# Memory rows issued from ScalarE and 64-row products as row pairs, in an interleaved two-block recurrent transformer kernel

## The chip, the cores and the metric

The kernel runs on one core of a Trainium2 chip. The metric is the device time of one execution in microseconds (us). The kernel before has a median of 1535.26 us over three runs (1532.87 to 1536.67). On this core TensorE multiplies matrices into PSUM (8 banks of 128 x 512 fp32), VectorE (DVE in the profile) and ScalarE (ACT) copy results out of PSUM and do the pointwise work, GpSimd (POOL) does a few small copies, and SyncE (SP) issues DMAs. Each engine runs its own list of instructions in order; semaphores order them between engines.

## The reference

The reference applies two blocks twice, x = x + A(layernorm(x)) and x = x + B(layernorm(x)), on 2048 rows of 448 numbers in bf16. Cut to what matters:

```python
def _A_ref(x, mem0, Wq, Wk, Wv, Wo, seg_len):          # 16 heads of 256, 8 memory rows, segments of 32
    mem = mem0
    for s in range(64):
        h = concat([mem, x[s*32:(s+1)*32]])            # 40 rows
        q, k, v = h @ Wq, h @ Wk, h @ Wv               # for each head
        p = softmax(where(mask, q @ k.T * scale, -1e9))
        o = (p @ v) @ Wo                               # summed over heads
        mem = o[:8]                                    # the next segment starts from these rows
        outs.append(o[8:])
def _B_ref(x, W_gate, W_up, W_down):                   # 448 -> 1792 -> 448
    return (relu(x @ W_gate) * (x @ W_up)) @ W_down
x = x + A(layernorm(x)); x = x + B(layernorm(x)); x = x + A(layernorm(x)); x = x + B(layernorm(x))
```

Block A is a recurrence over 64 segments: the memory rows of one segment are needed before the scores of the next can be formed.

## The kernel before, in words

At the start, for each head, the products M = Wq Wk^T and N = Wv Wo are formed and kept in SBUF, so that a segment needs T = h M, scores T h^T, a softmax, U = p h, and the output U N. The two applications of A run side by side as two layers, the second four segments (`LAG = 4`) behind the first. There are 68 steps, one for each segment; steps 0 to 3 and 64 to 67 have one layer, the others two. Step t does the following.

- `m_nat` (line 1203) copies the memory rows of the step before, which lie in `mv`, by DMA into `hK`, four DMAs of 8 rows x 224 (two layers, two halves; line 1216), and into `ride`, two DMAs of 16 rows x 224 (line 1223 adds them to the residual in every second step, on DVE). All six wait for `mv` alone. They are issued by `qdma` (line 893), which puts them on SP.
- `t_block` (line 982) forms T in 11 units of 4 to 6 head-columns, in three blocks of six, four and one unit. The 448 rows of the contraction are three tiles of 128 and one of 64. In the first two blocks the 64-row parts of all units come first (`first`, line 997), two units at a time: with two layers as four 64x64 products for each pair of columns (halves of rows times halves of columns), with one layer as two 64x128 products. Then come the 128-row parts of each unit (`rest`). Each unit fills one PSUM bank, which ACT or DVE empties by two copies, `TTm` (memory rows) and `TTs` (segment rows).
- `s_mem`, `p_t_mem`, `u_mem`, `un_mem` run the softmax, U and U N for the 8 memory rows only. Their result is `mv` (line 1178, DVE). `m_t` turns `mv` on TensorE, and DVE copies it to `hT`, where the next step's T reads it. This is the recurrence.
- `s_seg`, `seg_pt`, `u_seg` do the same for the 32 segment rows; `u_seg` ends in copies from PSUM to `U` (in the tile `big`) or `UTm`.
- In odd steps `un` forms the segment rows' output from `U`, `ln_b` normalises it (a DMA transpose `xBT<-xn` on SP is its last part), and `b_layer` runs block B.

The order of all work comes from a planner (`_Order.run`). Every operation gets a cost, a delay after its end (`lat`, in ns) and a due time. For TensorE operations the due time is looked up in a table `SLOT` that repeats every four steps. For the others it is worked back from the operations that follow, with corrections from `BIAS`. In the steady part (steps 8 to 63) the TensorE order is fixed by `SLOT` alone. The planner goes through time, gives each engine the operation that can start first (by due time where several can), chooses ACT or DVE for copies that may go to either, and assigns PSUM banks. Its costs for a DMA are 500 ns of SP and 2200 ns to landing for `qdma`, 120 ns of the issuing engine for the small loads that ACT issues at the start. Each engine's list is written out in this order and run strictly in it.

Of the kernel before, what the change touches and what calls it, by code (L numbers as in the profile page):

```python
# [24 lines left out]
DH = D // 2  # L25
# [508 lines left out]
def MM(out, lhsT, rhs, **kw):  # L534
    return (out, lhsT, rhs, kw)


class _Kernel:
# [354 lines left out]
    def qdma(self, name, fn, wr, rd=()):  # L893
        self.q.add("dma", ("sp",), {"sp": 500.0}, fn, rd, wr, name=name)

    def tile(self, pool, n):
        return _Tile(self, pool, n)

# [83 lines left out]
    def t_block(self, t, units):  # L982


        S = self
        pp, s = (t // 2) % 2, t % 2
        l0, l1 = S.layers(t)
        n = (l1 - l0) * KEYS
        rd = [("hTx", pp, s, l) for l in range(l0, l1)] + S.mkeys(pp, s, l0, l1) + (S.Mkeys if t == 0 else [])
        mov = lambda kt, h: S.hT[h, pp, kt, l0:l1, s, 0:KEYS]  # L990
        keys = lambda c, u0, m: [(nm, c, u0, half) for nm in ("TTm", "TTs") for half in ((0, 1) if c == 3 else (0,))]
        R = [S.tile("R", 1) for _ in units]
        pair = len(units) > 1
        block = str(S.BLOCKS.index(units))
        S.q.sub = block + "f"

        def first():
            out = []
            for a, b in zip(range(0, len(units), 2), range(1, len(units), 2)):
                for j in range(units[a][2]):  # L1000
                    for o, x in ((0, a), (0, b), (1, a), (1, b)) if l1 - l0 == 2 else ((-1, a), (-1, b)):
                        c, u0, m = units[x]
                        side, slot = S.PLACE[16 * c + u0 + j]
                        h, g = slice(64 * side, 64 * side + 64), slice(64 * o, 64 * o + 64) if o >= 0 else slice(0, 128)
                        out.append(MM(R[x].b()[g, j * n:j * n + n], S.M3[h, slot, g], mov(3, h), start=(j == 0), stop=False))
            return out

        if pair:
            S.mm(first, sum(u[2] for u in units[::2]) * S.pitch(n) + 25.0, rd, [r for x in R for r in x.res()] + [k for u in units for k in keys(*u)], mode=3 if l1 - l0 == 2 else 1)
        full = slice(0, 128)  # L1010
        for x, (c, u0, m) in enumerate(units):
            def rest(x=x, c=c, u0=u0, m=m):
                out = []
                for j in range(m):
                    v, o = R[x].b()[:, j * n:j * n + n], 16 * c + u0 + j
                    for kt in range(3):
                        out.append(MM(v, S.M[:, kt, o, :], mov(kt, full), start=(kt == 0 and not pair), stop=(kt == 2 and (j == m - 1 if pair else False))))
                    if not pair:
                        out.append(MM(v, S.M3[:, S.PLACE[o][1], :], mov(3, full), start=False, stop=True))
                return out  # L1020

            S.q.sub = block + "r"
            S.mm(rest, (3 if pair else 4) * m * S.pitch(n), rd, R[x].res() + ([] if pair else keys(c, u0, m)))
            S.t_copies(t, R[x], c, u0, m)
# [178 lines left out]
    def m_nat(self, t):  # L1203

        S = self
        pp, s = (t // 2) % 2, t % 2
        w = S.win(t - 1)
        for l in range(*S.layers(t)):
            if l == 1 and t == LAG:
                continue  # L1210
            for n in range(2):
                a, b = 64 * l + 32, 32 * n + 16 * w + 8 * l
                S.qdma(f"mk{l}{n}", lambda E, a=a, b=b, n=n: E.dma_start(S.hK[a:a + 8, pp, s, DH * n:DH * n + DH], S.mv[b:b + 8, :]),  # L1213
                       [("hKm", pp, s, l, n)], [("mem",)])
        S.q.sub = "x"
        p = (t - 2 - w) // 2
        if p in S.WTILES:
            for n in range(2):
                a, b = 64 + 16 * w, 32 * n + 16 * (1 - w)
                S.qdma(f"ride{n}", lambda E, a=a, b=b, n=n: E.dma_start(S.ride[a:a + 16, DH * n:DH * n + DH], S.mv[b:b + 16, :]), [("ride", w, n)], [("mem",)])  # L1220
            if w == 1:
                r = slice(64, 96)
                S.dve(lambda E: E.tensor_tensor(S.XB[r, (p + 1) % 2, :], S.ride[r, :], S.XA[r, p % 4, :], ALU.add), D,
                      [("ride", i, n) for i in range(2) for n in range(2)] + [("XA", p % 4, 1)], [("XB", (p + 1) % 2, 1)], base=(64, 64))
# [222 lines left out]
```

## Time and profile before

| | |
|---|---|
| median of 3 runs | 1535.26 us |
| the profiled execution | 1532.87 us, span 1531.1 us, mean granted TensorE clock 0.995 |
| PE busy | 1477.2 us, 41135 matmuls |
| DVE busy | 792.7 us |
| ACT busy | 784.5 us |
| DMAs `hK<-mv` and `ride<-mv` | 252 and 124, all issued from SP |

Busy time is the union of an engine's instructions. Instructions of a sequencer (marked with a q behind the engine, as in SPq) wait, branch or issue DMAs; they are not counted as busy. In a row of the timeline the first number is the start from the beginning of the span, the second the time that the merged instructions took, and what stands in brackets is how long the engine was idle before and what ended it.

### The profile page before, as it was taken

The page shows a single profiled execution, that of the slowest core. Times are in us where ns is not written, and L with a number is a line of the kernel's source. Part 1 is how long each engine was busy: PE and PEld are TensorE (multiplying, and loading weights), DVE is VectorE, ACT ScalarE, POOL GpSimd, SP SyncE. Part 2 cuts the span into 40 slices and gives each one's busy share as a digit, 9 for nine tenths or more (in the row PEclk, how much of TensorE's full clock was granted, in tenths as well). Part 3 has the DMA queues.
Part 4 walks back from the last instruction along what each step waited for, and adds up shares of the span by engine and source line. Part 5 has one row for each costly group of instructions (what it writes and reads, how often), then busy time and mean ns, then how long its engine had stood idle before and what let it go on. Part 6 is the DMA issues. An engine that isn't in the chain of part 4 may idle for free.

```text
span 1531.1 us, 88674 instructions
## 1 busy us (share of the span) xinstructions
PE 1477.2 (96%) x41135; PEld 1158.3 (76%) x41135; DVE 792.7 (52%) x2173; ACT 784.5 (51%) x2516; POOL 112.6 (7%) x259
## 2 busy tenths in 40 slices
PE   6999899999999999999999999999999999999998
PEld 2577777878787787878787787878788787878775
DVE  6544535545454555545555554545454564555554
ACT  6633554555545555554555455554555455554433
POOL 4000000000000000000000000000000000000000
PEclk9999999999999999999999999999999999999999
DMA  9741101111110100101010101111010110001010
GB/s 222 184 127 29 17 15 22 22 17 19 21 22 17 23 18 17 21 18 23 16 24 17 23 21 16 19 22 22 17 24 18 21 22 17 18 20 20 17 23 12
DMA packets 137761, 48.24 MB, mean 32 GB/s; under 512 B 125736, under 2 KB 137264, under 8 KB 137392
## 3 DMA queue, kind: packets, MB, share of 16 engines
q1 hardware_dynamic: 137040, 42.33, 14.2%
q8 instruction: 323, 5.29, 1.5%
q14 instruction: 46, 0.38, 0.1%
q10 hardware_dynamic: 352, 0.24, 0.1%
HBM read 10.33 MB, written 1.84 MB: 8 GB/s over the span
## 4 chain that ended last, share of the span: by engine, by line
PE 80%; DVE 8%; DMA 5%; SPq 4%; ACT 2%; issue 1%
PE b L139 80%; DMA xBT<-xn 3%; SPq L692 3%; DVE UTm L867 1%; DMA PTs<-Ps 1%; DVE big L867 1%; ACT Em L1071 1%; SPq L1213 1%; DVE stat L1115 1%; DVE mv L1178 1%; DVE Ps L1117 1%; DMA ride<-mv 0%; ACT Es L1114 0%; DVE stat L1112 0%; ACT sumA L866 0%
## 5 line engine op out<-in xcount | busy, mean ns | idle before, releaser
L139 PE MATMUL b<-hT,Mw 128*128 128x80 bf16 (+1 forms) x11424 | 440.4, 200 | 7.3 <-issue 5.7
L139 PEld LDWEIGHTS b<-hT,Mw 128*128 128x128 bf16 x11424 | 420.7, 100 | 24.6 <-issue 8.7
L139 PE MATMUL b<-Nw,big 128*32 128x448 bf16 (+1 forms) x3924 | 298.9, 353 | 1.0 <-DMA Nw<-in_A_Wo_dram 1.0
L866 ACT ACTIVATE TTs<-b 128x320 bf16<-128x320 f32 (+5 forms) x666 | 282.2, 424 | 3.6 <-PE b L139 3.5
L866 ACT ACTIVATE TTm<-b 128x80 bf16<-128x80 f32 (+5 forms) x667 | 155.8, 234 | 248.0 <-PE b L139 241.8
L139 PE MATMUL b<-xBT,big 128*128 128x128 bf16 (+3 forms) x4900 | 213.1, 216 | 5.3 <-DMA xBT<-xn 4.9
L139 PEld LDWEIGHTS b<-Nw,big 128*32 128x32 bf16 (+1 forms) x3924 | 129.5, 97 | 100.0 <-issue 10.3
L139 PEld LDWEIGHTS b<-xBT,big 128*128 128x128 bf16 (+1 forms) x4900 | 185.6, 102 | 22.9 <-DMA xBT<-xn 6.9
L139 PE MATMUL b<-Nw,UTm 128*32 128x224 bf16 x7504 | 194.0, 261 | 3.8 <-ACT UTm L866 1.6
L139 PEld LDWEIGHTS b<-Nw,UTm 128*32 128x32 bf16 x7504 | 176.6, 97 | 24.1 <-issue 10.8
L867 DVE CAST TTm<-b 64x64 bf16<-64x64 f32 (+5 forms) x217 | 47.5, 219 | 201.6 <-PE b L139 198.9
L866 ACT ACTIVATE big<-b 128x512 bf16<-128x512 f32 (+1 forms) x214 | 110.1, 566 | 75.8 <-PE b L139 75.4
L139 PE MATMUL b<-hT,M 64*64 64x80 bf16 (+3 forms) x6808 | 145.2, 199 | 1.5 <-DVE hT L867 0.8
L867 DVE CAST big<-b 128x512 bf16<-128x512 f32 (+1 forms) x174 | 98.4, 587 | 74.4 <-PE b L139 74.4
L139 PEld LDWEIGHTS b<-hT,M 64*64 64x64 bf16 (+2 forms) x6808 | 110.9, 107 | 26.9 <-issue 12.1
L867 POOL COPY hK<-xn 32x448 bf16<-32x448 bf16 x136 | 75.1, 552 | 588.0 <-DVE xn L920 581.8
L1344 ACT ACTIVATE gT<-b 128x512 bf16<-128x512 f32 (+1 forms) x128 | 66.9, 543 | 89.2 <-PE b L139 51.7
L866 ACT ACTIVATE UTm<-b 128x512 bf16<-128x512 f32 (+2 forms) x159 | 83.6, 555 | 51.0 <-PE b L139 49.1
L139 PE MATMUL b<-big,hB 128*128 128x448 bf16 (+1 forms) x574 | 100.9, 353 | 0.7 <-DVE hB L1345 0.7
L1345 DVE TENSOR_TENSOR hB<-gT,b 128x512 bf16<-128x512 bf16 (+2 forms) x128 | 79.3, 620 | 37.5 <-PE b L139 17.8
L867 DVE CAST TTs<-b 64x256 bf16<-64x256 f32 (+4 forms) x218 | 88.4, 406 | 3.1 <-PE b L139 3.0
L866 ACT ACTIVATE sumA<-b 64x224 f32<-64x224 f32 x67 | 23.7, 353 | 114.2 <-PE b L139 114.2
(101 smaller groups left out, 1331.7 us busy)
## 6 DMA issues: line engine op xcount, KB each, us to landing
hK<-mv SPq DMA_DIRECT2D x252, 3.5 KB
big<-in_A_Wo_dram SPq DMA_DIRECT2D x3, 896.0 KB, 5.7
ride<-mv SPq DMA_DIRECT2D x124, 7.0 KB, 1.8
out_dram<-ys SPq DMA_DIRECT2D x32, 56.0 KB, 2.0
big<-in_B_W_up_dram SPq DMA_DIRECT2D x7, 224.0 KB, 3.1
big<-in_B_W_gate_dram SPq DMA_DIRECT2D x7, 224.0 KB, 3.8
big<-in_B_W_down_dram SPq DMA_DIRECT2D x7, 224.0 KB, 3.6
XA<-in_A_x_dram SPq DMA_DIRECT2D x28, 56.0 KB, 2.3
```

The lines of the kernel that those rows point to most:

```text
L139: ins = E.matmul(out, lhsT=lhsT, rhs=rhs, **kw)
L692: S.q.add("dma", ("sp",), {"sp": 6200.0 if w == "Wv" and q else 4100.0}, lambda E: E.dma_start_transpose(out=st[w, q], in_=src[w][:, q * 1 ...
L866: return E.activation(out(), src(), ACT.Copy, **({} if scale is None else {"scale": scale}))
L867: return E.tensor_copy(out(), src()) if scale is None else E.tensor_scalar(out(), src(), scale, None, op0=ALU.mult)
L1071: S.act(lambda E, i=i: E.activation(S.Em[:, i, :], src()[:, i, :], ACT.Exp, bias=st[:, 32 + i:33 + i], scale=1.0, accum_out=st[:, 34 + i:3 ...
L1115: S.dve(lambda E: E.tensor_reduce(st[:, 48:48 + n], Es, AX.X, ALU.add), w, [("Es",)], [("ss", 1)])
L1117: S.dve(lambda E: E.tensor_tensor(dst, Es, bc(56), ALU.mult), w, [("Es",), ("ss", 2)], [("Ps",)])
L1178: S.dve(lambda E: E.tensor_tensor(S.mv[0:64, :], C.b()[0:64, 0:DH], S.sumA[:, :], ALU.add), DH, C.res(half=(0,)) + [("sumA",)], [("mem",)])
L1213: S.qdma(f"mk{l}{n}", lambda E, a=a, b=b, n=n: E.dma_start(S.hK[a:a + 8, pp, s, DH * n:DH * n + DH], S.mv[b:b + 8, :]), [("hKm", pp, s, l, ...
L1344: S.act(lambda E, g=g, R=R, n=n: E.activation(S.gT[:, g, 0:n], R[0].b()[:, 0:n], ACT.Relu), n, R[0].res(), [("gT", g)])
L1345: S.dve(lambda E, g=g, R=R, n=n, fcs=fcs: E.tensor_tensor(S.hB[:, fcs[0]:fcs[-1] + 1, 0:w], S.gT[:, g, 0:n].rearrange("p (a b) -> p a b", ...
```

## The change

The two kinds of DMA of `m_nat` go through a new helper `adma`, which puts them on ACT's list instead of SP's, with a planner cost of 120 ns of ACT and 2200 ns to landing. In `t_block` the 64-row parts are two 64x128 products for each pair of columns whatever the number of layers; with two layers they were four 64x64 products. The tables `SLOT` and `BIAS` are the same in both kernels; the planner works the order out anew.

```diff
+    def adma(self, name, fn, wr, rd=()):
+        self.q.add("dma", ("act",), {"act": 120.0}, fn, rd, wr, name=name, lat=2200.0)
...
-                    for o, x in ((0, a), (0, b), (1, a), (1, b)) if l1 - l0 == 2 else ((-1, a), (-1, b)):
+                    for x in (a, b):
                         c, u0, m = units[x]
                         side, slot = S.PLACE[16 * c + u0 + j]
-                        h, g = slice(64 * side, 64 * side + 64), slice(64 * o, 64 * o + 64) if o >= 0 else slice(0, 128)
-                        out.append(MM(R[x].b()[g, j * n:j * n + n], S.M3[h, slot, g], mov(3, h), start=(j == 0), stop=False))
+                        h = slice(64 * side, 64 * side + 64)
+                        out.append(MM(R[x].b()[:, j * n:j * n + n], S.M3[h, slot, :], mov(3, h), start=(j == 0), stop=False))
...
-            S.mm(first, sum(u[2] for u in units[::2]) * S.pitch(n) + 25.0, rd, [r for x in R for r in x.res()] + [k for u in units for k in keys(*u)], mode=3 if l1 - l0 == 2 else 1)
+            S.mm(first, sum(u[2] for u in units[::2]) * S.pitch(n) + 25.0, rd, [r for x in R for r in x.res()] + [k for u in units for k in keys(*u)], mode=1)
...
-                S.qdma(f"mk{l}{n}", lambda E, a=a, b=b, n=n: E.dma_start(S.hK[a:a + 8, pp, s, DH * n:DH * n + DH], S.mv[b:b + 8, :]),
+                S.adma(f"mk{l}{n}", lambda E, a=a, b=b, n=n: E.dma_start(S.hK[a:a + 8, pp, s, DH * n:DH * n + DH], S.mv[b:b + 8, :]),
                        [("hKm", pp, s, l, n)], [("mem",)])
...
-                S.qdma(f"ride{n}", lambda E, a=a, b=b, n=n: E.dma_start(S.ride[a:a + 16, DH * n:DH * n + DH], S.mv[b:b + 16, :]), [("ride", w, n)], [("mem",)])
+                S.adma(f"ride{n}", lambda E, a=a, b=b, n=n: E.dma_start(S.ride[a:a + 16, DH * n:DH * n + DH], S.mv[b:b + 16, :]), [("ride", w, n)], [("mem",)])
```

## The prediction

> **What bounds the kernel now.** I read the page first, then the waits of TensorE in the steady part (190 to 1420 us), then the rows of the tile `mv`, then the timeline around single steps. The page (busy time, slices, DMA issues):
>
> ```profile
> PE 1477.2 (96%) x41135; PEld 1158.3 (76%) x41135; DVE 792.7 (52%) x2173; ACT 784.5 (51%) x2516; POOL 112.6 (7%) x259
> ...
> PEclk9999999999999999999999999999999999999999
> ...
> hK<-mv SPq DMA_DIRECT2D x252, 3.5 KB
> ...
> ride<-mv SPq DMA_DIRECT2D x124, 7.0 KB, 1.8
> ```
>
> TensorE's waits between 190 and 1420 us (total, times, longest):
>
> ```profile
> PE b L139 <- issue: 5.1, 12, 0.8
> PE b L139 <- DMA xBT<-xn: 3.0, 7, 1.3
> PE b L139 <- DVE mv L1178: 2.7, 13, 0.2
> ```
>
> TensorE is busy 96% of the span at full clock and waits some 15 us in 1230. Its order in this part is a fixed list, so a copy that comes late is a hole that nothing fills; and there is hardly a wait to win back. What the steps' copies have in hand decides what the change costs.
>
> What an issue costs, from the rows of `mv` on SP (shortest, median, longest in ns) and from the only issues that ACT makes, in the timeline's first microseconds:
>
> ```profile
> L1213 SPq DMA_DIRECT2D hK<-mv x252: 624/651/1443, 77.8 to 1500.6; - x126
> L1220 SPq DMA_DIRECT2D ride<-mv x124: 517/583/1572, 173.1 to 1499.3; - x124
> ```
>
> ```profile
> 2.02 0.73 ACTq L707 DMA_DIRECT2D ys<-in_A_mem_dram  x1
> 2.79 0.28 ACTq L708 DMA_DIRECT2D ys<-in_A_mem_dram  x1
> 3.10 1.12 ACTq L831 DMA_DIRECT2D XA<-in_A_x_dram  x2
> ```
>
> An issue holds its queue for about 0.6 us on either engine; the planner is told 0.12. Last, the timeline of ACT behind two `mv` (they end at 848.61 and 893.72 by the rows of DVE):
>
> ```profile
> 850.03 0.38 ACT L866 ACTIVATE big<-b 128x256 bf16<-128x256 f32 x1
> ...
> 850.74 0.24 ACT L866 ACTIVATE TTm<-b 128x80 bf16<-128x80 f32 x1 [0.33 <-PE b L139]
> ```
>
> ```profile
> 895.74 0.38 ACT L1344 ACTIVATE gT<-b 128x256 bf16<-128x256 f32 x1 [2.44 <-DVE hB L1345]
> 896.15 0.24 ACT L866 ACTIVATE TTm<-b 128x80 bf16<-128x80 f32 x1
> ...
> 897.89 0.43 ACT L866 ACTIVATE TTs<-b 128x320 bf16<-128x320 f32 x1
> ```
>
> The copies of T begin about 2.1 to 2.4 us after `mv` there, and from then on ACT runs without a gap. The last one ends at 898.32, and TensorE's next 64-row block, which fills six banks at once, begins at 898.51: 0.2 us in hand.
>
> **The six DMAs, from SP to ACT.** Six issues hold ACT for 4 x 0.651 + 2 x 0.583 = 3.77 us a step; in all 252 x 0.651 + 124 x 0.583 = 236 us. They wait for `mv` alone, and their due time (the next step's `u_mem` less 2.3 us and the correction of 5.0) lies ahead of the T copies', so the planner sends them as soon as `mv` is there, for 0.72 us by its own reckoning. Behind them on ACT stand the copies that follow `mv`, and TensorE waits for the banks and tiles of these. The work before repeats every four steps (86.9 us from the `mv` at 848.61 to the one at 935.54), so I take four `mv` in turn, with lateness at the first copy less the idle time of ACT before it and what it has in hand:
>
> - A, `mv` at 848.61: ACT is full from 848.17 to about 853.2 except 0.33 us. 3.77 - 0.33 - 0.2 in hand = 3.2 us.
> - B, 871.71: ACT idles to 872.79, then two copies of `U` for `un`, then 4.35 us of idle. The first starts 871.75 + 3.77 - 872.79 = 2.7 late. TensorE reads it 32 matmuls of 0.047 behind 872.78, at 874.3, 0.9 after its end at 873.39. 1.8 us. The T copies that follow have the 4.35 and are on time.
> - C, 893.72: ACT idles to 895.74. 893.76 + 3.77 - 895.74 = 1.8 late, 0.2 in hand: 1.6 us.
> - D, 911.99: four copies of `U` till 913.89, then 3.50 us of idle before the T copies. 3.77 - 3.50 gives 0.3; the `U` copies put behind the issues have 2.3 us in hand. 0.3 us.
>
> Sum 6.9 us in 86.9. The 56 steady steps hold 14 such fours: 97 us. Outside them are 376 - 336 = 40 issues, 25 us; at the same share (6.9 of 15.1 us of issues) 12 us.
>
> Bounds: ACT's own rows run from 0.28 to 0.73 an issue. With 0.28 (1.7 us a step) only A is late, 1.2 us: 14 x 1.2 + 5 = 22 us. With 0.73 (4.4) the four are 3.8, 2.4, 2.2, 0.7: 14 x 9.1 + 18 = 145. I take SP's medians, since they are of the same transfers, and the ACT row that is nearest to them (8 rows of 896 bytes, 0.73) is longer, not shorter.
>
> **What the ride addition waits for.** DVE's addition (line 1223) waits for `ride` 80.4 us in 30 times already. The planner placed it 6 x 0.5 + 2.2 = 5.2 us behind `mv`; it will place it 0.7 + 2.2 = 2.9 behind. The rows land 3.77 + 1.8 = 5.6 behind. So DVE can stand for up to 2.7 us more with copies behind it, 28 times in the steady part: 0 to 76 us, part of it beside ACT's lateness. I take 10, as in A and C DVE has its T copies 5.3 us or more behind `mv` now.
>
> **SP without them.** SP loses the same 3.77 us a step. Behind them stood the transposes for `xBT` and `PTs` and the loads of x. TensorE's waits for these are 3.0 and 0.2 us in the steady part: 0 to 3 us won; I take 0. `hK` itself is read by `u_mem` and `u_seg` many microseconds on, and no wait for it is in the list: 0 either way.
>
> The Trainium skill, page "DMA: Bandwidth & Descriptors", section "Issuing engines are not separate DMA queues", says that issuing from several engines saves only the sequencer's time, usually small against the transfer. Here that time is not small: 0.65 beside 1.8 us to landing. By the rule the move would be worth nothing either way and the sum would end at 1535; by the rows the sequencer's time is the whole price, because ACT has other work.
>
> **The row pairs.** Two 64x128 products take the place of four 64x64 ones; 25 pairs of columns a step, 60 steps with two layers. Rows of the timeline: sixty 64x64 products of 80 columns took 0.73 us, the last one 0.20, so (0.73 - 0.20) / 59 = 9.0 ns each, 36 for four; full products of 80 columns go at 36 too. Thirty 64x128 products of 40 columns (one-layer steps) took 0.54, the last 0.18: 12.4 each, 25 a pair, which is also the pace of full products of 40 columns. A pair thus keeps the pace of one full product and I take 36 for 36: 0 us. Were the two halves to follow one another, 25 x 36 ns x 60 = 54 us would come on top. The switch into and out of the smaller tiles is about 0.13 us by the 40 and 60 quads (0.48 and 0.67 to the next start), 0.11 behind the pairs of 40 columns: at best 0.02 x 120 = 2 us won. 3000 matmuls and as many weight loads fall away, beside others.
>
> **Sum.** 97 + 12 + 10 + 0 + 0 = 119 on the profiled execution's 1532.9 gives 1652; the median of before lies 2.4 above that execution: 1654.
>
> **Rivals.**
> 1. Not slower: ACT is idle for 49% and the issues fit there. It speaks for it that a step has some 10 us of idle ACT, against it that the planner believes in 0.12 us and puts all six right behind `mv`. It decides if an issue takes ACT 0.25 us or less: then six take 1.5 us and C, B, D lose nothing, A loses 1.0 at most, or nothing where DVE takes a copy. Time: 1535 less the 3 us of SP and the 0.5% of the span (8 us) that the chain of waits gives to `ride<-mv`, 1524 to 1536.
> 2. The ride addition blocks DVE in full: 14 fours x 2 x 2.7 = 76, in place of 10: 1720.
> 3. The pairs do not overlap: 1654 + 54 = 1708.
> 4. Issues at ACT's lower row: 1535 + 22 = 1557.
>
> The skill's page "TensorE: Matmul & The Clock Gate", Part 1, says that an idle window of about 3.4 us halves the clock. The granted clock here is 0.995 and TensorE has no such gap, so no row shows it; if A's 3.2 us tripped it, an estimate by that page is half of 3.4 us lost each time, 14 x 1.7 = 24 us more.
>
> **How the numbers follow.** The sum as worked out 0.63, rival 1 0.05, rival 2 0.14, rival 3 0.06, rival 4 0.12. The range runs from between rival 4 and the sum, 1585, to rival 2, 1720; outside it are rival 1, most of rival 4 and a little above. A measurement tells about 0.3% (5 us) from no change. Slower by more: all but rival 1, 0.94 with rounding of its upper end; the same 0.02; faster 0.04.
>
> **What would show it.** Right: `hK<-mv` and `ride<-mv` stand as ACTq at about 0.6 us each, directly behind `mv`; TensorE's waits for ACT `TTm`, `TTs` and `big` grow from next to nothing to some 100 us, in stretches of 2 to 3 us in the four places; PE busy falls below 92%; the four steps take 93 to 95 us in place of 86.9; 64x128 products of 80 columns at 18 ns each. Wrong: issues of 0.3 us or less; T copies that start as early behind `mv` as now; waits for ACT that stay under 20 us, or the same lateness met by DVE taking the copies; a pair at 72 ns.

## The result and the profile after

The kernel after takes 1695.05 us (median of four runs, 1690.79 to 1698.62) against 1534.68 for the kernel before, taken beside it: a ratio of 1.104 with a 95% interval of 1.101 to 1.108. It is 160 us slower; 119 were predicted, and the result lies inside the range.

The page after (busy time, the chain that ended last, DMA issues):

```profile
PE 1520.3 (90%) x38135; PEld 1189.2 (70%) x38135; DVE 795.0 (47%) x2176; ACT 779.6 (46%) x2513; POOL 112.6 (7%) x259
...
PE 67%; ACTq 10%; DVE 9%; ACT 6%; DMA 3%; SPq 3%; issue 2%
...
hK<-mv ACTq DMA_DIRECT2D x252, 3.5 KB
...
ride<-mv ACTq DMA_DIRECT2D x124, 7.0 KB, 1.8
```

Before, PE was busy for 1477.2 us of a span of 1531.1; now it is busy for 1520.3 of 1690.4. So the 159.3 us that the span has gained are 116.2 us of an idle TensorE and 43.1 us of a TensorE that takes longer over its matmuls, 3000 fewer than before. The two parts have different causes, and the split is the first thing to take from the page. ACT's own work has hardly changed (784.5 to 779.6): what holds it, ACTq, does not count as busy, but it is now 10% of the chain.

The mean granted clock names the second part. It was 0.995 before:

```profile
core 0: 1690.4 us, clock 0.966
```

In the trace the clock is either 1.0 or 0.5; it is at 0.5 for 118.2 us in all, in stretches of 3.41 us or twice that (before: 16.7 us). Half of the difference, 51 us, is the work that was lost, if TensorE has work at the time.

TensorE's waits in the steady part (200 to 1570 us; total, times, longest) name the first part:

```profile
PE b L139 <- ACT UTm L866: 52.3, 14, 4.0
PE b L139 <- ACT big L866: 34.5, 25, 2.6
PE b L139 <- ACT TTs L866: 26.0, 14, 3.4
...
PE b L139 <- DMA xBT<-xn: 0.2, 1, 0.2
```

None of the three ACT waits was among the main waits before. The first comes 14 times at 3.7 us, once in each four steps. The issues themselves (lines 1216 and 1223 here, 1213 and 1220 in the kernel before) cost what they cost on SP (shortest, median, longest in ns):

```profile
L1216 ACTq DMA_DIRECT2D hK<-mv x252: 631/652/2037, 78.2 to 1655.7; - x126
L1223 ACTq DMA_DIRECT2D ride<-mv x124: 514/607/1575, 175.8 to 1654.4; - x124
```

Where the four places of the prediction are in the code: A is the step with `t % 4 == 1`, B 2, C 3 and D 0. The timeline at A, where `mv` ends at 923.17:

```profile
922.72 0.59 ACT L866 ACTIVATE UTm<-b 128x512 bf16<-128x512 f32 x1
...
923.21 2.78 ACTq L1216 DMA_DIRECT2D hK<-mv  x4
...
926.01 1.18 ACTq L1223 DMA_DIRECT2D ride<-mv  x2
...
927.24 0.60 ACT L866 ACTIVATE UTm<-b 128x512 bf16<-128x512 f32 x1 [3.93 <-DVE XB L1293]
...
927.98 0.53 PE L139 MATMUL b<-hT,M 64*128 64x80 bf16 x20 [3.72 <-ACT UTm L866]
```

The six issues stand 0.04 us behind `mv` and hold ACT for 3.98 us. A copy to `UTm` that empties a bank stands behind them, and TensorE's second 64-row block, which needs that bank, waits for 3.72 us. (The releaser in ACT's brackets is an operation that ended before; what held ACT is in the rows of ACTq above it.) At C, where `mv` ends at 975.11, the same thing hits the `gT` copy ahead of the T copies:

```profile
975.14 2.68 ACTq L1216 DMA_DIRECT2D hK<-mv  x4
...
980.02 0.38 ACT L1347 ACTIVATE gT<-b 128x256 bf16<-128x256 f32 x1 [5.32 <-issue]
...
980.30 0.23 ACT L866 ACTIVATE TTm<-b 128x80 bf16<-128x80 f32 x1
```

What follows a long gap is the slower part. Two windows behind the gap at A (length, then busy time and instructions of PE, PEld, DVE, ACT and POOL, then the granted clock, the DMA share and GB/s):

```profile
924.20:928.00 3.80, 0.08 (x6) 0.05 (x3) 2.56 (x5) 0.76 (x2) 0.00 (x0) 1.00 0.09 23
928.00:931.40 3.40, 3.40 (x73) 3.34 (x74) 0.63 (x2) 2.40 (x9) 0.00 (x0) 0.66 0.02 5
931.40:934.80 3.40, 3.40 (x93) 3.27 (x91) 0.73 (x4) 2.10 (x8) 0.00 (x0) 0.83 0.21 43
```

TensorE is full in the second and third window, but it gets through 73 and 93 matmuls. A mean clock of 0.66 is half clock in 0.68 of the window, and 0.83 in 0.34 of it, so the clock is at 0.5 for 0.68 x 3.4 + 0.34 x 3.4 = 3.5 us of the two.

The fixed order allows a sharper account. TensorE runs the same 2352 groups of matmuls in the steady part of both kernels, in the same order, so the time from the start of one group to the start of the next can be subtracted pair by pair. The steady part (steps 8 to 63) goes from 1253.1 to 1402.7 us, +149.6:

| in the steady part, 14 times each | us in all | us each |
|---|---|---|
| A, ahead of the second 64-row block | 54.4 | 3.9 |
| B, inside `un` | 32.1 | 2.3 |
| C, ahead of the first 64-row block | 27.8 | 2.0 |
| D, ahead of the second 64-row block | 6.4 | 0.5 |
| slower work in the T blocks behind A and C | 27.6 | 2.0 |
| everything else | about 1 | |

### The profile page after: what moved, and what is told of

Its sections match the earlier page's. It is cut to its first block, busy times and chain, and to the rows that moved or that the text cites. A ratio compares the mean times of both kernels' runs of the same rounds, so it can differ in the third digit from the quotient of the medians.

```text
span 1690.4 us, 82676 instructions
## 1 busy us (share of the span) xinstructions
PE 1520.3 (90%) x38135; PEld 1189.2 (70%) x38135; DVE 795.0 (47%) x2176; ACT 779.6 (46%) x2513; POOL 112.6 (7%) x259
## 4 chain that ended last, share of the span: by engine, by line
PE 67%; ACTq 10%; DVE 9%; ACT 6%; DMA 3%; SPq 3%; issue 2%
PE b L139 67%; ACTq L1216 7%; ACTq L1223 3%; SPq L692 3%; DMA PTs<-Ps 2%; DVE big L867 2%; ACT TTs L866 1%; ACT big L866 1%; DVE mv L1181 1%; DVE UTm L867 1%; ACT sumA L866 1%; ACT Em L1074 1%; DVE hB L1348 1%; ACT UTm L866 1%; ACT TTm L866 1%
## 5 line engine op out<-in xcount | busy, mean ns | idle before, releaser
L139 PE MATMUL b<-hT,Mw 128*128 128x80 bf16 (+1 forms) x11424 | 468.4, 205 | 1.4 <-DVE M L867 1.2
L139 PEld LDWEIGHTS b<-hT,Mw 128*128 128x128 bf16 x11424 | 450.2, 103 | 19.0 <-DVE M L867 1.6
L139 PE MATMUL b<-Nw,big 128*32 128x448 bf16 (+1 forms) x3924 | 308.1, 361 | 32.5 <-ACT big L866 31.5
L866 ACT ACTIVATE TTm<-b 128x80 bf16<-128x80 f32 (+5 forms) x665 | 159.6, 240 | 228.8 <-PE b L139 222.7
L139 PE MATMUL b<-hT,M 64*128 64x80 bf16 (+3 forms) x3808 | 153.8, 202 | 88.1 <-ACT UTm L866 52.3
L139 PEld LDWEIGHTS b<-hT,M 64*128 64x128 bf16 (+1 forms) x3808 | 112.6, 100 | 116.8 <-issue 57.9
L867 DVE CAST TTm<-b 64x64 bf16<-64x64 f32 (+4 forms) x219 | 48.0, 219 | 262.5 <-PE b L139 260.2
L1348 DVE TENSOR_TENSOR hB<-gT,b 128x512 bf16<-128x512 bf16 (+2 forms) x128 | 79.2, 620 | 41.4 <-PE b L139 20.1
L139 PE MATMUL b<-PTs,hK 40*64 40x512 bf16 (+1 forms) x1024 | 76.5, 361 | 9.2 <-DMA PTs<-Ps 5.5
```

Source lines behind the costliest of these rows:

```text
L139: ins = E.matmul(out, lhsT=lhsT, rhs=rhs, **kw)
L866: return E.activation(out(), src(), ACT.Copy, **({} if scale is None else {"scale": scale}))
L867: return E.tensor_copy(out(), src()) if scale is None else E.tensor_scalar(out(), src(), scale, None, op0=ALU.mult)
L1348: S.dve(lambda E, g=g, R=R, n=n, fcs=fcs: E.tensor_tensor(S.hB[:, fcs[0]:fcs[-1] + 1, 0:w], S.gT[:, g, 0:n].rearrange("p (a b) -> p a b", ...
```

## The experiments

All ratios are against the kernel before, run beside the experiment on the same chip, where its median lay between 1529.4 and 1536.7 us; the expectations are in us on a base of about 1535, so differences of a few us are read from the ratios. "Busy" and "idle" are PE's busy time and the rest of the span; the kernel before has 1477.2 and 53.9.

**The move alone, and the row pairs alone.** The first keeps the four 64x64 products, the second keeps the DMAs on SP.

```diff
# move_only, against the kernel before
-                S.qdma(f"mk{l}{n}", lambda E, a=a, b=b, n=n: E.dma_start(S.hK[a:a + 8, pp, s, DH * n:DH * n + DH], S.mv[b:b + 8, :]),
+                S.adma(f"mk{l}{n}", lambda E, a=a, b=b, n=n: E.dma_start(S.hK[a:a + 8, pp, s, DH * n:DH * n + DH], S.mv[b:b + 8, :]),
-                S.qdma(f"ride{n}", lambda E, a=a, b=b, n=n: E.dma_start(S.ride[a:a + 16, DH * n:DH * n + DH], S.mv[b:b + 16, :]), [("ride", w, n)], [("mem",)])
+                S.adma(f"ride{n}", lambda E, a=a, b=b, n=n: E.dma_start(S.ride[a:a + 16, DH * n:DH * n + DH], S.mv[b:b + 16, :]), [("ride", w, n)], [("mem",)])
# pairs_only, against the kernel after
-                S.adma(f"mk{l}{n}", lambda E, a=a, b=b, n=n: E.dma_start(S.hK[a:a + 8, pp, s, DH * n:DH * n + DH], S.mv[b:b + 8, :]),
+                S.qdma(f"mk{l}{n}", lambda E, a=a, b=b, n=n: E.dma_start(S.hK[a:a + 8, pp, s, DH * n:DH * n + DH], S.mv[b:b + 8, :]),
-                S.adma(f"ride{n}", lambda E, a=a, b=b, n=n: E.dma_start(S.ride[a:a + 16, DH * n:DH * n + DH], S.mv[b:b + 16, :]), [("ride", w, n)], [("mem",)])
+                S.qdma(f"ride{n}", lambda E, a=a, b=b, n=n: E.dma_start(S.ride[a:a + 16, DH * n:DH * n + DH], S.mv[b:b + 16, :]), [("ride", w, n)], [("mem",)])
```

> The six DMAs on ACT, the 64-row parts still as four 64x64 products. Theory (ACT's time): everything comes from the issues, 1690 to 1700 us, TensorE's granted clock 0.965 to 0.97. Rival (the pairs share in the cost): 1640 to 1680.

> The row pairs alone, DMAs on SP as before. Theory: 1533 to 1537 us, 64x128 products of 80 columns at 18 ns each. Rival (the pairs share in the cost): 1545 to 1590.

Measured: the move alone 1696.43 us, 1.105 [1.100, 1.110], busy 1521.0, idle 169.0. The row pairs alone 1531.59 us, 0.997 [0.995, 0.999], busy 1473.9, idle 54.1. The whole loss is the move. The pairs are a small gain, which had been put at nothing. The rows of the products, before and with pairs alone:

```profile
L139 PE MATMUL b<-hT,M 64*64 64x80 bf16 x6000 | 77.9, 200 | 1.1 <-issue 0.5 <-DVE hT L867 0.4
```

```profile
L139 PE MATMUL b<-hT,M 64*128 64x80 bf16 x3000 | 74.5, 199 | 0.5 <-DVE hT L867 0.4
```

Half as many products take 3.4 us less, which is the 3.3 us that PE's busy time loses. So two row pairs do overlap (the 54 us of that rival are not there), and they gain 0.3%. In TensorE's waits the 5.1 us of "issue" of the kernel before are gone as well; but the idle total is the same, so how much of the gain is fewer instructions and how much the pace of the products is not told apart.

**What holds ACT: time alone, or the DMAs?** The DMAs stay on SP. For each of them ACT gets a copy of 128x512 into a tile that nothing reads, which waits for `mv` and which the planner is told takes 120 ns.

```diff
+    def hold(self, i):
+        self.q.add("op", ("act",), {"act": 120.0}, lambda E, e: E.activation(self.junk[:, :], self.M[:, 0, 0:4, :].rearrange("p a b -> p (a b)"), ACT.Copy), [("mem",)], [("hold", i)])
...
                        [("hKm", pp, s, l, n)], [("mem",)])
+                S.hold(0)
```

> Row pairs, DMAs on SP; for each DMA of memory or riding rows ACT makes an extra copy of 128x512 to a scratch tile that waits for the memory rows too and costs 120 ns in the planner. It moves nothing that anyone reads: the work is left in, and 376 copies are added. Theory (what costs is that ACT is held behind the memory rows, by whatever): copies of about 0.55 us, 3.4 us a step, 1650 to 1695 us. Rival (queues, transfers or the ride addition that waits on DVE): 1533 to 1550.

Measured: 1618.4 us, 1.053 [1.049, 1.057], busy 1489.6, idle 131.3. This lies 32 us under the theory's range. The copies took the time of the issues (the row of `junk`: shortest, median, longest), and TensorE waits for ACT at the same kinds of copies, but not at `UTm`:

```profile
L901 ACT ACTIVATE junk<-Mw x376: 618/630/655, 79.4 to 1589.2; 128x512 bf16<-128x512 bf16 x188
```

```profile
PE b L139 <- ACT TTs L867: 43.7, 27, 1.9
PE b L139 <- ACT big L867: 24.9, 16, 1.9
PE b L139 <- ACT UTm L867: 2.5, 12, 0.2
```

A load on ACT that has nothing to do with DMA thus gives half the loss. The other half is put down to position, which was read from the timeline and not tested by a run of its own. The issues have readers (`u_mem` and the ride addition) and so an early due time; the copies into `junk` have none, so the planner lets ready copies go between them. The timeline of ACT shows it:

```profile
899.62 0.63 ACT L901 ACTIVATE junk<-Mw 128x512 bf16<-128x512 bf16 x1
900.14 0.39 ACT L867 ACTIVATE big<-b 128x256 bf16<-128x256 f32 x1
900.40 1.30 ACT L901 ACTIVATE junk<-Mw 128x512 bf16<-128x512 bf16 x2
901.61 0.22 ACT L867 ACTIVATE TTm<-b 128x80 bf16<-128x80 f32 x1
```

By the group-by-group account, no place loses more than 2.1 us: 1.9 ahead of A's first 64-row block, 2.1 inside `un`, 1.5 at C, nothing at D, and only 0.4 ahead of A's second block, where the kernel after loses 3.9. Between the two profiled executions, 39 us are idle time (170.1 against 131.3) and 31 are TensorE's own slower work (1520.3 against 1489.6), as there is less half clock too (48.3 us against 118.2).

**The planner's order alone.** The order of the kernel after is kept, and SP emits the DMAs in their places.

```diff
-                self.sc.dma(o.name, o.fn, res(o.rd), res(o.wr), eng=o.fixed)
+                self.sc.dma(o.name, o.fn, res(o.rd), res(o.wr), eng="sp" if o.cat == "m_nat" else o.fixed)
```

> The order of every engine as in the changed kernel, but the six DMAs are issued by SP in that order. Theory (ACT's time): the late copies are gone, 1533 to 1550 us, where DVE may wait longer for the riding rows since the order believes in 120 ns. Rival (the new order itself is what is worse): 1650 to 1695.

Measured: 1544.0 us, 1.0059 [1.0037, 1.0081], busy 1477.5, idle 62.5. With the same order and no issue on ACT, 151 of the 160 us are gone. ACT, DVE and GpSimd run their instructions in exactly the order of the kernel after (their sequences in the two traces are the same). So it is the issues' time on ACT, in that order, and not the order as such. What is left stands behind the DMAs on SP, which that order was not made for:

```profile
PE b L139 <- DMA xBT<-xn: 9.9, 8, 2.4
```

**Four issues, or two.** In one kernel only the memory rows go through ACT, in the other only the riding rows.

```diff
# hk_on_act, against the kernel after
-                S.adma(f"ride{n}", lambda E, a=a, b=b, n=n: E.dma_start(S.ride[a:a + 16, DH * n:DH * n + DH], S.mv[b:b + 16, :]), [("ride", w, n)], [("mem",)])
+                S.qdma(f"ride{n}", lambda E, a=a, b=b, n=n: E.dma_start(S.ride[a:a + 16, DH * n:DH * n + DH], S.mv[b:b + 16, :]), [("ride", w, n)], [("mem",)])
# ride_on_act, against the kernel after
-                S.adma(f"mk{l}{n}", lambda E, a=a, b=b, n=n: E.dma_start(S.hK[a:a + 8, pp, s, DH * n:DH * n + DH], S.mv[b:b + 8, :]),
+                S.qdma(f"mk{l}{n}", lambda E, a=a, b=b, n=n: E.dma_start(S.hK[a:a + 8, pp, s, DH * n:DH * n + DH], S.mv[b:b + 8, :]),
```

> Only the four memory-row DMAs on ACT, riding rows on SP, row pairs kept. Theory (lateness at the first tight copy, what is in hand taken off once): four issues hold ACT 2.7 us in place of 4.0, so the four places fall from 3.9, 2.3, 2.0, 0.5 to 2.6, 1.0, 0.7, 0.5 us, 4.8 x 14 = 67, 7 outside, no idle stretch that reaches the clock: 1600 to 1620 us, clock 0.985 or more. Rival (a price for each issue, wherever it stands): two thirds of 160 us, 1642.

> Only the two riding-row DMAs on ACT, memory rows on SP, row pairs kept. Theory: 1.2 us of ACT, late only at the place without idle time (1.0 to 1.2 us, 14 times), 2 outside: 1545 to 1556 us. Rival (a price for each issue): a third of 160 us, 1588.

Measured: four issues a step 1605.72 us, 1.0486 [1.0454, 1.0518], busy 1491.1, idle 103.9; two issues a step 1539.01 us, 1.0059 [1.0041, 1.0077]. The first lies in the theory's range, the second 6 us under it; the kernel before took 1529.37 us on this chip, so they are 76 and 10 us slower. At A the delay is 1.1 us with two issues, 2.6 with four, 3.9 with six: 0.55 to 0.65 us an issue, all of it paid. At B it is about 0, 0.9 and 2.3, at C about 0, 0.4 and 2.0: there the first issues are covered by ACT's idle time, and only what goes over it is paid. TensorE's wait at A, with four issues and with two:

```profile
PE b L139 <- ACT UTm L866: 34.0, 14, 2.8
```

```profile
PE b L139 <- ACT UTm L866: 12.9, 14, 1.3
```

With four issues the gap at A is 2.4 us in most fours, which the expectation took to be too short for the clock; it halved behind 8 of the 14. What goes with it can be read from the trace. All stretches of half clock begin on one raster of 3413 ns, and two neighbouring gaps of 2.4 us fall differently into it. The gap of 332.8 to 335.2 lies almost wholly in one window of the raster (first row), and the next window has half clock (second row). The gap of 425.9 to 428.3 is shared by two windows, and the clock stays full in the window behind them (last row):

```profile
331.46:334.87 3.41, 1.30 (x31) 0.36 (x29) 3.13 (x8) 0.81 (x2) 0.19 (x1) 1.00 0.05 9
334.87:338.28 3.41, 3.12 (x56) 3.04 (x57) 0.90 (x2) 1.87 (x7) 0.00 (x0) 0.50 0.06 17
423.63:427.04 3.41, 2.29 (x44) 0.76 (x36) 2.98 (x6) 1.32 (x3) 0.19 (x1) 1.00 0.03 6
427.04:430.46 3.42, 2.13 (x67) 2.10 (x68) 1.82 (x4) 2.56 (x8) 0.00 (x0) 1.00 0.10 24
430.46:433.87 3.41, 3.41 (x110) 3.28 (x107) 1.28 (x6) 2.76 (x13) 0.00 (x0) 1.00 0.63 41
```

TensorE was busy for 1.30 us of the first window (38%), and for 2.29 and 2.13 us of the two that share the other gap (67 and 62%). Behind the first gap it does 56 matmuls in 3.12 busy us at half clock, behind the second 110 in 3.41 at full clock.

**One place at a time.** ACT issues only in the steps of A, or only in those of D.

```diff
-                S.adma(f"mk{l}{n}", lambda E, a=a, b=b, n=n: E.dma_start(S.hK[a:a + 8, pp, s, DH * n:DH * n + DH], S.mv[b:b + 8, :]),
+                (S.adma if t % 4 == 1 else S.qdma)(f"mk{l}{n}", lambda E, a=a, b=b, n=n: E.dma_start(S.hK[a:a + 8, pp, s, DH * n:DH * n + DH], S.mv[b:b + 8, :]),
-                S.adma(f"ride{n}", lambda E, a=a, b=b, n=n: E.dma_start(S.ride[a:a + 16, DH * n:DH * n + DH], S.mv[b:b + 16, :]), [("ride", w, n)], [("mem",)])
+                (S.adma if t % 4 == 1 else S.qdma)(f"ride{n}", lambda E, a=a, b=b, n=n: E.dma_start(S.ride[a:a + 16, DH * n:DH * n + DH], S.mv[b:b + 16, :]), [("ride", w, n)], [("mem",)])
```

> All six on ACT, but only in every fourth step, the one whose copies leave ACT no idle time (t modulo 4 is 1); elsewhere SP. Theory: 54 us of stall and 21 us of halved clock behind it, 1600 to 1618 us. Rival (a price for each issue): a quarter of 160 us, 1575.

> All six on ACT, but only in every fourth step, the one where ACT idles 3.5 us behind its copies (t modulo 4 is 0); elsewhere SP. Theory: 6 us, 1536 to 1545 us. Rival (a price for each issue): 1575.

Measured: A alone 1607.81 us, 1.0512 [1.0487, 1.0537], busy 1502.6, idle 101.0; D alone 1534.47 us, 1.0031 [1.0016, 1.0045], 1.5 us under its range. Against the 1529.37 us of the kernel before on this chip, the same number of issues costs 5 us in one place and 78 in another. A's 78 are 53.9 of delay and 22.5 of slower T blocks behind it. TensorE's wait at A alone:

```profile
PE b L139 <- ACT UTm L866: 51.8, 14, 4.0
```

**No idle window at A.** The kernel after with twelve matmuls of 512 columns put into TensorE's order ahead of the second 64-row block of A. Their results are overwritten.

```diff
+        if pair and block == "1" and t % 4 == 1 and 2 * LAG <= t < NSEG:
+            S.q.sub = "1w"
+            S.mm(lambda: [MM(R[0].b()[:, 0:512], S.ident[:, :], S.M[:, 0, 0:4, :], start=True, stop=True) for _ in range(12)], 30.0, rd, R[0].res())
+            S.q.sub = "1f"
```

> The changed kernel with twelve idle matmuls of 512 columns (2.6 us, into the first bank of the block, written over afterwards) ahead of the block that waits at the first place, in the 14 steady steps. Theory (the gap of 3.9 us halves the clock for the work behind it): the stall stays, the clock does not fall there, some 20 us less, 1668 to 1685 us. Rival (the slower work behind it has another cause): 1690 to 1700; up to 1731 if the matmuls come on top.

Measured: 1659.8 us, 1.0789 [1.0745, 1.0834], 35 us less than the kernel after, although TensorE has some 35 us more to do: the group of products of this shape has 41.4 us, of which 6.8 are 26 products that the kernel after has too. The mean granted clock is 0.988. TensorE's waits:

```profile
PE b L139 <- ACT big L866: 33.8, 25, 2.8
PE b L139 <- ACT TTs L866: 27.9, 15, 2.6
PE b L139 <- ACT UTm L866: 13.0, 14, 1.0
```

The waits at B, C and D are as they were; the one at A is down to 0.9 us. Idle time falls by 36.2 us (170.1 to 133.9), about what the filling takes up, and the gain is in TensorE's own work: 1520.3 busy before the filling, 1527.8 - 41.4 + 6.8 = 1493.2 with it, 27 us less. (The two profiled executions are 28.7 us apart, the medians 35.) By groups, the T blocks behind A are 24.6 us shorter. The direction was expected, the size (20) was too small, and the time fell under its range. This shows that the half clock behind A is caused by the gap: the six issues have stayed where they were. One thing beside the filling changed, as the planner worked the order out anew: one `TTm` copy in nearly every four steps went from ACT to DVE (ACT runs 13 instructions fewer, DVE 13 more).

**The planner told the true price.** Only the two numbers in `adma` are changed.

```diff
-        self.q.add("dma", ("act",), {"act": 120.0}, fn, rd, wr, name=name, lat=2200.0)
+        self.q.add("dma", ("act",), {"act": 650.0}, fn, rd, wr, name=name, lat=1800.0)
```

> The changed kernel with the planner told what an issue takes, 650 ns of ACT and 1800 to landing; the table of places is as it was. Theory (ACT's time where it has none to spare): the order can move copies to DVE but ACT stays full at the first place, 1620 to 1690 us. Rival (the order was misled, a true price mends it): 1535 to 1560.

Measured: 1553.14 us, 1.0107 [1.0069, 1.0145], busy 1482.7, idle 73.6. The theory as it was put (the time on ACT is lost whatever the planner believes) missed by 67 us, and its rival (the order was misled) was right. The page and TensorE's waits:

```profile
PE 1482.7 (95%) x38131; PEld 1159.2 (74%) x38135; DVE 885.9 (57%) x2427; ACT 703.5 (45%) x2262; POOL 111.6 (7%) x259
```

```profile
PE b L139 <- ACT TTs L866: 8.5, 11, 2.1
PE b L139 <- DVE UTm L867: 6.4, 15, 1.2
```

In the steady part some 225 of the copies that either engine can make went from ACT to DVE. At A the issues still stand right behind `mv`, but `UTm` is copied by DVE beside them, and the two riding rows wait till later:

```profile
864.08 2.69 ACTq L1216 DMA_DIRECT2D hK<-mv  x4
...
864.73 0.68 DVE L867 CAST UTm<-b 128x512 bf16<-128x512 f32 x1
...
865.47 0.53 PE L139 MATMUL b<-hT,M 64*128 64x80 bf16 x20 [0.33 <-DVE UTm L867]
...
866.80 0.55 ACTq L1223 DMA_DIRECT2D ride<-mv  x1
```

TensorE waits 0.33 us there instead of 3.72. By the ratios (1.104 and 1.011), 144 of the 160 us were the wrong price, and 16 us are what the issues cost on ACT when the copies are shared out with them in mind.

**Another engine as issuer.** ACT and SP are both out of it: GpSimd (busy 7%) issues the six DMAs, priced at 1000 ns, once with the row pairs and once with the four 64x64 products.

```diff
-        self.q.add("dma", ("act",), {"act": 120.0}, fn, rd, wr, name=name, lat=2200.0)
+        self.q.add("dma", ("pool",), {"pool": 1000.0}, fn, rd, wr, name=name, lat=2200.0)
```

> The six DMAs issued by GpSimd, which is 7% busy, planned at 1000 ns each; row pairs kept. Theory (what costs is the issuer's other work): nothing is late, 1530 to 1545 us, more only if riding rows land later than 6 us behind the memory rows. Rival (a second queue costs in itself): 1600 or more.

> The six DMAs issued by GpSimd, planned at 1000 ns, the 64-row parts as four 64x64 products as before. GpSimd and row pairs together gave 0.993, the pairs alone 0.997. Theory (two separate gains: fewer instructions, and SP's transposes no longer behind the issues): 0.995 to 0.998 of the time before. Rival (all of it from the pairs): 0.999 to 1.002. Rival (all from the issuer): 0.992 to 0.994.

Measured: with row pairs 1526.04 us, 0.9930 [0.9904, 0.9956], 4 us under its range and faster than both kernels; with the 64x64 products 1528.35, 0.9986 [0.9973, 0.9998], which falls between the range of the theory and that of the first rival. The issue takes POOL 0.52 and 0.49 us, and the waits for `xBT` behind SP's DMAs go from 3.0 to 0.7 us:

```profile
L1216 POOL DMA_DIRECT2D hK<-mv x252: 518/518/649, 81.5 to 1495.5; - x126
L1223 POOL DMA_DIRECT2D ride<-mv x124: 484/490/518, 176.6 to 1491.9; - x124
```

```profile
PE b L139 <- DMA xBT<-xn: 0.7, 2, 0.3
```

The pairs gave 0.29% alone, GpSimd gives 0.14% alone. The sum, 0.43%, lies just outside the interval of both together (0.44 to 0.96%), but the two have intervals of their own (0.12 to 0.47 and 0.02 to 0.27%). Whether the 0.27% on top is real isn't settled, and the gain from GpSimd alone is barely off nothing.

## Why the prediction came out as it did

It was right in sign, mechanism and places, and 41 us too low. Its steps in turn:

- *Six issues at SP's medians.* Right: 0.652 and 0.607 us on ACT against the 0.651 and 0.583 taken. The bound from ACT's row of 0.28 us (rival 4, 1557) did not occur, nor did rival 1: ACT's idle half did not help, since the issues stand 0.03 to 0.04 us behind `mv`, as foreseen.
- *A, 3.2 us: measured 3.9.* The 0.33 us of idle time and the 0.2 in hand were taken off for the chain of T copies. What TensorE waited for was the `UTm` copy, tight behind `mv`, which has neither: nearly the whole 3.98 us is paid. (The 0.2 in hand is besides a reading at C; A's rows do not show it.) The place was right and the copy was another one; the list of what would show it did not have `UTm`.
- *B, 1.8: measured 2.3. C, 1.6: measured 2.0. D, 0.3: measured 0.5.* The right size each, a few tenths low. In the step from 951.29 on, the six issues take 3.9 us at B with the gaps between them, not 3.77. At C in the timeline shown, the two riding rows took 2.12 us (975.14 to 979.97 for all six).
- *97 us of waiting in the steady part, 12 outside.* TensorE's idle time in the steady part went from 1230 - 1212.8 = 17.2 us (190 to 1420) to 1370 - 1245.8 = 124.2 (200 to 1570): +107. The whole span has +116.2, so 9 fall outside. (The 12 should have been 11, as 25 x 6.9 / 15.1 = 11.4; and of the upper bound, D with 4.4 us of issues is 0.9 and not 0.7, which makes 148 of the 145. Neither bears on the result.)
- *The ride addition, 10 us.* Not there as an extra: DVE's wait for `ride` is 80.4 us before and 81.2 after. Rival 2 (1720) fell with it.
- *SP without the DMAs, 0; row pairs, 0.* The wait for `xBT` went from 3.0 to 0.2 us, the pairs gained 3. Both lie in the bounds. Rival 3 (a pair at 72 ns) did not occur.

97 + 12 + 10 = 119 predicted stands against 116 us of idle time measured. That the two lie so near is in part luck: the delays at the four places are 120.7 us in the table above and not 97, while the 10 us of the ride addition did not come. **The failed step is the term that the sum left out: the halved clock.** It cost 43 us of busy time, or 46 against the kernel with row pairs alone, and with it 116 + 43 = 159. The prediction had named it and left it outside because no row of the kernel before showed such a gap in the steady part; but its own figure for A, 3.2 us, was already the length of the gap that would have to be priced. By the filling at A, 25 us (the T blocks behind A) to 27 us (all of TensorE's work) of it come from there.

The Trainium skill, page "TensorE: Matmul & The Clock Gate", Part 1, has the clock halved after an idle window of about 3.4 us, in windows of 3413 ns that run on their own. The runs agree on the 3.41 us stretches and on a raster, which lies differently against the kernel's start in each trace, and the estimate by it, 24 us for A, was the right order (22.5 behind A with A alone). They differ on how long the gap must be: here a window that was idle for a little more than half was enough (see the last section).

What was on the list as the shape of the result: PE busy below 92% (90%), waits for ACT copies of some 100 us (112.8). Four steps were to take 93 to 95 us and took 98.0 (from the `mv` that ends at 923.17 to the one that ends at 1021.14): 11.1 us more than before in place of 6.9. By the table above, 2.0 us of this are the slower work, which the 6.9 did not have, and 1.7 are what the four places cost above their sum. The cause of the waits was put as the issues' time; the run with the planner's true price adds that most of that time could have been laid beside other work, had the planner known of it. The prediction noted both prices (0.12 and 0.6) and did not ask what the planner would do with the right one.

## What to carry to other kernels

A DMA issue is work of the engine that issues it, about 0.65 us here for 3.5 KB, and it goes into a planner's prices like any copy: the same six issues cost 160 us at a price of 0.12 and 16 at the true one. Before moving issues to an engine with half its time free, look at what stands right behind the event that they wait for, since the loss is the time by which those copies start late, and the engine's mean load says nothing of it. When a predicted hole in TensorE's work comes near 2 us or more, price the slower work behind the hole as well; here it was a quarter of the loss, and holes of 1.9 us and more had it.

## What the runs showed of the hardware

- *The clock halves behind gaps shorter than 3.4 us, and not each time.* Counted in the granted clock of the steady part: with ACT issuing only at A, all 14 gaps of 3.6 to 4.0 us were followed by half clock, 8 of them for 6.8 us; with four issues, 8 of the 14 gaps of 2.4 to 2.8 us; with the copies in place of the issues, 3 of the 28 gaps of 1.9 us. What goes with it in a single case is how much of one raster window the gap takes. In each of the 14 kept traces all stretches of half clock begin on one raster of 3413 ns (within 3 ns). Counted over all of them, from 200 us to 120 us before the end: of the windows at full clock, all 75 in which TensorE was busy for less than 44% were followed by half clock, 9 of the 47 with 44 to 50% were, and 3 of the 4940 with more. A window at half clock was followed by a second one in all 21 cases in which TensorE was busy for less than 79.5% of it, and in none with more. A gap of 1.9 us is 55% of a window and halves the clock only if nearly all of it falls into one; a gap of 3.9 us takes at least 57% of one of the windows that it touches, wherever it falls. This is a count made afterwards; no run moved a gap along the raster on purpose.
- *Issues stretch.* The median is 0.65 us on SP and on ACT, but single ones took up to 1.44 and 1.57 us on SP and 2.04 on ACT. On GpSimd the longest was 0.65. What stretches them stays open.
- *GpSimd issues these transfers as fast as the others:* 0.52 and 0.49 us, with 2.1 and 1.9 us to landing for 3.5 and 7.0 KB; on ACT 7.0 KB took 1.8.
- *Two 64x128 products in the place of four 64x64 ones* of 80 columns keep at least the same pace: 74.5 us for 3000 against 77.9 for 6000.
